# Decode attention with a gated feed-forward: tile slots numbered by the program, w_down in one load, sixteen single-partition loads on GpSimd's queue

## The chip, the cores and the metric

One core of a Trainium2 chip runs the whole kernel. The metric is the device time of one execution in microseconds; the median of three runs is given, and beside it one execution that was taken with the hardware profiler.

## What is computed

One token attends over a cache of 65,536 keys and values in each of 32 heads, and a feed-forward of the same token is mixed in with a gate:

```
q = x @ wq                        # x: 1 x 512, wq: 512 x 4096, 32 heads of 128
p = softmax(q . k_cache / sqrt(128))     # k_cache: 32 x 65536 x 128, bf16
a = (p @ v_cache) @ wo            # wo: 4096 x 512
b = (silu(x @ w_gate) * (x @ w_up)) @ w_down    # 512 x 1792, 1792 x 512
g = sigmoid(sum(x * gate_w))
out = g * a + (1 - g) * b
```

The two caches are 1,073.7 MB of the 1,087.6 MB that the kernel reads from HBM.

## The kernel before, in words

**Tiles.** A head's keys are cut into G = 4 tiles of 128 x 128 positions, so there are N = 128 K tiles and as many V tiles, of 4 MiB each: 128 partitions with 32 KB each, contiguous in HBM. They live in the pool `ring` (L58), which has SLOTS = 5 buffers under one tag; `big` (L69) takes the next one. The same five slots first hold wq (L77), K0, K1, w_gate with w_up (L132) and w_down (L136), and at the end the second half of wo (`load_wo_end`, L157). The first half of wo comes in four groups of four heads from a pool of its own (`load_wo`, L164).

**Engines.** For a K tile, DVE multiplies it in place by the query, which is broadcast along the positions (L240), and halves the products three times by adding (L244) down to 16 columns; `scores` (L249) sums those on PE with 16 matmuls against an identity (L254). After a head's four tiles come the maximum (L266 to L275), the exponentials on ACT (L279) and their total (L288). `values` (L296) multiplies a V tile by the probabilities in 32 matmuls of 4 columns each (L302). `head_column` (L320) turns a head's result into a column, and `project` (L334) multiplies it by its 128 rows of wo into a_ps.

**Order.** It is written out by hand. `steps` (L344) pairs each K tile n with a V tile v: v starts four tiles behind n and from n = 40 on falls back to eight behind. In a step the program issues the load of K tile n and then that of V tile v, both on SP's queue, then DVE's products of K tile n, and on PE, in this order, the column of a finished head, `values` of v, the total, `scores` of n, and the projection of a finished head. An engine carries out its instructions in that order, and SP issues a load only when what it waits for has come: the slot's earlier users, and an earlier load that used the same one of eight DMA semaphores. A DMA's semaphore is raised by one by each of the DMA engines that carry it, sixteen for a whole tile. The last steps hold V tiles only; the last two V tiles and the second half of wo are loaded in pieces, so that PE can begin on the first.

**Feed-forward.** `feed_forward_in` (L169) is issued in step 1, `feed_forward_mid` (L189) in step 2 and `feed_forward_out` (L218) in step 3. w_down lies in 64 partitions with 28 KB each. It comes in eight loads of eight rows, every fourth one (`load_wd`, L142): two of them stand ahead of the load of K2 on SP's queue, six behind it. The hidden vector is brought into the same 64-partition form by two matmuls (L202) and a copy (L206), and b_ps takes 28 matmuls (L209).

Of the kernel before, what the change touches and what calls it, by code (L numbers as in the profile page):

```python
# [8 lines left out]
ACT = mybir.ActivationFunctionType  # L9
ALU = mybir.AluOpType  # L10
AXIS = mybir.AxisListType
P = 128
# [3 lines left out]
NB = 128  # L16
SLOTS = 5
# [8 lines left out]
def kernel(  # L26
# [14 lines left out]
    nc = tc.nc  # L41
    bf16 = mybir.dt.bfloat16
    f32 = mybir.dt.float32

    _, H, Sk, Dh = A_k_cache.shape
    D = A_x.shape[2]
    F = B_w_gate.shape[1]
    KT = D // P
    FT = F // P
    G = Sk // (NB * P)  # L50
    NBH = Sk // P
    N = H * G
# [2 lines left out]
    scale = float(Dh) ** -0.5  # L55

    consts = ctx.enter_context(tc.tile_pool(name="consts", bufs=1))
    ring = ctx.enter_context(tc.tile_pool(name="ring", bufs=SLOTS))  # L58
    small = ctx.enter_context(tc.tile_pool(name="small", bufs=2))
    ppool = ctx.enter_context(tc.tile_pool(name="ppool", bufs=3))  # L60
    wo_pool = ctx.enter_context(tc.tile_pool(name="wo_pool", bufs=2))
# [3 lines left out]
    psum_m = ctx.enter_context(tc.tile_pool(name="psum_m", bufs=2, space=bass.MemoryType.PSUM))  # L65

    ctx.enter_context(tc.manual_schedule())

    def big(name):  # L69
        return ring.tile([P, NB * Dh], bf16, name=name, tag="big")  # L70


    xT = consts.tile([P, KT], bf16, name="xT")
    gwT = consts.tile([P, KT], bf16, name="gwT")
    with nc.allow_non_contiguous_dma(reason="small"):
        nc.scalar.dma_start(out=xT, in_=A_x[0, 0, :].rearrange("(p t) -> p t", t=KT))
    wq_t = big("wq_t")  # L77
    wq_sb = wq_t[:, : KT * H * Dh].rearrange("p (t f) -> p t f", t=KT)
    nc.sync.dma_start(out=wq_sb, in_=A_wq.rearrange("(p t) f -> p t f", t=KT))

    ident_f = consts.tile([P, P], f32, name="ident_f")
    make_identity(nc, ident_f[:])
    ident_b = consts.tile([P, P], bf16, name="ident_b")
# [15 lines left out]

    K_tiles, V_tiles, S_tiles, P_tiles, O_tiles = {}, {}, {}, {}, {}  # L100

    def load(dst, cache, n, name, cuts=(0, NB)):
        h, g = divmod(n, G)
        t = big(name)
        view = t.rearrange("p (j d) -> p j d", d=Dh)
        src = cache[0, h, g * NB * P : (g + 1) * NB * P, :].rearrange("(p j) d -> p j d", j=NB)
        for a, b in zip(cuts[:-1], cuts[1:]):
            nc.sync.dma_start(out=view[:, a:b, :], in_=src[:, a:b, :])
        dst[n] = view

    load(K_tiles, A_k_cache, 0, "K_t", (0, NB // 2, NB))
    load(K_tiles, A_k_cache, 1, "K_t")

    def queries(g):
        qg_ps = psum_m.tile([P, QG * Dh], f32, name="qg_ps", tag="misc")
# [13 lines left out]
        queries(g)  # L129


    gu_t = big("gu_t")  # L132
    wgu_sb = gu_t[:, : 2 * KT * F].rearrange("p (w t f) -> p w t f", w=2, t=KT)
    nc.sync.dma_start(out=wgu_sb[:, 0], in_=B_w_gate.rearrange("(p t) f -> p t f", t=KT))
    nc.sync.dma_start(out=wgu_sb[:, 1], in_=B_w_up.rearrange("(p t) f -> p t f", t=KT))
    wd_t = big("wd_t")  # L136
    HP = P // 2
    GT = F // HP
    wd_sb = wd_t[:HP, : GT * D].rearrange("p (t n) -> p t n", t=GT)
    wd_rows = B_w_down.rearrange("(p t) n -> p t n", t=GT)  # L140

    def load_wd(*which):  # L142
        for i in which:
            lo = (0, 1, 2, 3, 32, 33, 34, 35)[i]
            part = slice(lo, lo + 29, 4)
            nc.sync.dma_start(out=wd_sb[part], in_=wd_rows[part])

    with nc.allow_non_contiguous_dma(reason="small"):
        nc.sync.dma_start(out=gwT, in_=gate_w.rearrange("(p t) -> p t", t=KT))
    load_wd(0, 1)  # L150
    WG = 4
    wo_tiles = {}

    WH = H // 2
    wo_end = []

    def load_wo_end(cuts):  # L157
        t = big("wo_t")[:, : (H - WH) * D].rearrange("p (h n) -> p h n", n=D)
        rows = A_wo[WH * P :, :].rearrange("(h p) n -> p h n", p=P)
        for a, b in zip(cuts[:-1], cuts[1:]):  # L160
            nc.sync.dma_start(out=t[:, a:b, :], in_=rows[:, a:b, :])
        wo_end.append(t)

    def load_wo(g):  # L164
        wo_tiles[g] = wo_pool.tile([P, WG, D], bf16, name="wo_sb")
        rows = A_wo[g * WG * P : (g + 1) * WG * P, :]
        nc.sync.dma_start(out=wo_tiles[g], in_=rows.rearrange("(h p) n -> p h n", p=P))

    def feed_forward_in():  # L169

# [18 lines left out]
    def feed_forward_mid(gu_sb, eg):  # L189
        nc.vector.tensor_scalar_add(eg, eg, 1.0)  # L190
        nc.vector.reciprocal(eg, eg)
        hprod = consts.tile([P, FT], f32, name="hprod")
        nc.vector.tensor_tensor(out=hprod, in0=gu_sb[:, :FT], in1=eg, op=ALU.mult)
        hT = consts.tile([P, FT], bf16, name="hT")
        nc.vector.tensor_tensor(out=hT, in0=hprod, in1=gu_sb[:, FT:], op=ALU.mult)
        xg = consts.tile([P, KT], f32, name="xg")
        nc.vector.tensor_tensor(out=xg, in0=xT, in1=gwT, op=ALU.mult)
        xs = consts.tile([P, 1], f32, name="xs")
        nc.vector.tensor_reduce(out=xs, in_=xg, axis=AXIS.X, op=ALU.add)
        h_ps = psum_m.tile([HP, GT], f32, name="h_ps", tag="misc")  # L200
        for r in range(2):
            nc.tensor.matmul(  # L202
                h_ps[:, r * FT : (r + 1) * FT], lhsT=ident_b[:, r::2], rhs=hT, start=True, stop=True
            )
        h2 = consts.tile([HP, GT], bf16, name="h2")
        nc.scalar.activation(out=h2, in_=h_ps, func=ACT.Copy)  # L206
        b_ps = psum_m.tile([1, D], f32, name="b_ps", tag="misc")
        for t in range(GT):
            nc.tensor.matmul(  # L209
                b_ps, lhsT=h2[:, t : t + 1], rhs=wd_sb[:, t, :], start=(t == 0), stop=(t == GT - 1)  # L210
            )
        g_ps = psum_m.tile([P, 1], f32, name="g_ps", tag="misc")
        nc.tensor.matmul(g_ps, lhsT=ones_f, rhs=xs, start=True, stop=True)
        eg2 = consts.tile([P, 1], f32, name="eg2")
        nc.scalar.activation(out=eg2, in_=g_ps, func=ACT.Exp, scale=-1.0)
        return b_ps, eg2
# [13 lines left out]
    def products(n, a=0, b=NB):  # L230

        h = n // G
        K = K_tiles[n][:, a:b, :]
        qb = q_bc[:, h * Dh : (h + 1) * Dh]
        q_rep = bass.AP(
            tensor=qb.tensor,
            offset=qb.offset,
            ap=[list(qb.ap[0]), [0, b - a], [1, Dh]],
        )
        yield nc.vector.tensor_tensor(out=K, in0=K, in1=q_rep, op=ALU.mult)  # L240
        half = Dh
        while half > WIDTH:
            half //= 2
            yield nc.vector.tensor_tensor(  # L244
                out=K[:, :, 0:half], in0=K[:, :, 0:half], in1=K[:, :, half : 2 * half],
                op=ALU.add,
            )
# [97 lines left out]
    v = 0  # L345
# [8 lines left out]
    ff = done = tot_ps = None  # L354
    for n, v in steps:
        if n is not None and n > 1:
            load(K_tiles, A_k_cache, n, "K_t")
        if n == 2:
            load_wd(2, 3, 4, 5, 6, 7)
        if n == 3:  # L360
            load_wo(0)
        if v is not None:
            if v % (WG * G) == 2 * G and v // (WG * G) + 1 < WH // WG:
                load_wo(v // (WG * G) + 1)
            load(V_tiles, A_v_cache, v, "V_t", (0, NB) if v < N - 2 else (0, 64, NB) if v < N - 1 else (0, 32, 64, 96, 112, NB))
            if v == N - 1:
                load_wo_end((0, 4, 8, 12, 14, 16))
        if n == 2:
            ff = feed_forward_mid(*ff)
        halves = (0, NB // 2)  # L370
        vector = iter(()) if n is None else products(n)
        if n == 0:
            vector = (i for a in halves for i in products(n, a, a + NB // 2))
        top_of = None
        if n is None:
            top_of = H - 1 if S_tiles else None
        elif n % G == 0 and n > 0:
            top_of = n // G - 1
            vector = (i for a in halves for i in products(n, a, a + NB // 2))
        if top_of is not None:  # L380
            next(vector, None)
            mT_ps = row_max(top_of)
            next(vector, None)
            exponentials(top_of, mT_ps)
        for _ in vector:
            pass
        if n == 1:
            ff = feed_forward_in()
        if n == 3:
            feed_forward_out(*ff)  # L390
        if tot_ps is not None:
            weight(*tot_ps)
            tot_ps = None
        if done is not None:
            head_column(done, head_copy(done))
        if v is not None:
            values(v)
        if top_of is not None:
            tot_ps = top_of, total(top_of)
        if n is not None:  # L400
            scores(n)
        if done is not None and done < WH:
            project(done)
        done = v // G if v is not None and v % G == G - 1 else None
# [40 lines left out]
```

## Time and profile before

| what | us |
|---|---|
| median of three runs | 2533.54 (2533.16 to 2534.53) |
| the profiled execution's own time | 2534.51 |
| its span, first to last instruction | 2532.6 |
| DVE busy | 2175.5 |
| PE busy, matmuls | 1742.4 |
| ACT busy | 75.9 |
| GpSimd busy | 0.7 |

The page gives the busy time of each engine, the queues of the DMA engines with the share of the sixteen engines' time that their packets took, and the chain of work that ended last. q1 is the queue that SP issues to, q10 that of ACT, and q8 carries the instructions that the engines' sequencers fetch. GpSimd issues no DMA in this kernel. The page's mean rate is 430 GB/s. A table by stage gives the same for stretches of the span, and a timeline the instructions in order of time. In these a line such as `SPq L108` is the issue of a load by SP, not its transfer.

### The profile page before, as it was taken

To read this page: it belongs to the slowest core of one execution; us is meant where nothing else is said; L and a number is where in the kernel's file an instruction comes from. 1 tells how busy PE (TensorE), PEld (TensorE's weight loads), DVE (VectorE), ACT (ScalarE), POOL (GpSimd) and SP (SyncE) were. 2 spreads that over 40 slices of the span, in tenths; PEclk is the share of its full clock that TensorE was granted. 3 is DMA by queue.
4 is the path that set the end of the run, shared out by engine and by line. 5 is a ranking of instruction groups with operands and counts; after the bars stand their busy time and mean duration, and the time that the engine had idled before them with its cause. 6 is when DMAs were issued, how large, how long until landed. Compare 5 with 4: busy or idle time off the path is not lost.

```text
span 2532.6 us, 15260 instructions
## 1 busy us (share of the span) xinstructions
PE 1742.4 (69%) x6738; PEld 712.1 (28%) x6738; DVE 2175.5 (86%) x784; ACT 75.9 (3%) x207; POOL 0.7 (0%) x6
## 2 busy tenths in 40 slices
PE   4677666776677666676776677667666776677679
PEld 2222222222222222222222223222222232222223
DVE  7998888888888999998888888888888888888860
ACT  1000000000000000000000000000000000000000
POOL 0000000000000000000000000000000000000000
PEclk7677777777777676677777777777777777777779
DMA  9999999999999999999999999999999999999998
GB/s 415 433 433 430 433 433 433 432 430 435 432 432 434 431 433 432 432 433 433 432 434 433 432 434 433 432 432 434 432 431 434 433 430 434 434 431 433 434 432 339
DMA packets 42884, 1088.63 MB, mean 430 GB/s; under 512 B 4737, under 2 KB 8834, under 8 KB 9090
## 3 DMA queue, kind: packets, MB, share of 16 engines
q1 hardware_dynamic: 42674, 1087.66, 99.7%
q8 instruction: 53, 0.87, 0.1%
q14 instruction: 13, 0.11, 0.0%
q10 hardware_dynamic: 144, 0.00, 0.0%
HBM read 1087.64 MB, written 0.00 MB: 429 GB/s over the span
## 4 chain that ended last, share of the span: by engine, by line
DMA 68%; PE 22%; DVE 10%; issue 1%; ACT 0%; DVEq 0%; SPq 0%
DMA V_t<-in_A_v_cache_dram 61%; PE O_ps L302 20%; DMA K_t<-in_A_k_cache_dram 5%; DVE K_t L240 5%; DVE K_t L244 5%; PE S_ps L254 1%; DMA wo_t<-in_A_wo_dram 1%; DMA wq_t<-in_A_wq_dram 0%; PE qg_ps L117 0%; DVE m L266 0%; PE oh_ps L323 0%; PE a_ps L335 0%; PE a_ps L227 0%; ACT P_sb L279 0%; DVE top L275 0%
## 5 line engine op out<-in xcount | busy, mean ns | idle before, releaser
L302 PE MATMUL O_ps<-V_t,P_sb 128*4 128x512 bf16 x4096 | 1157.3, 453 | 496.8 <-DMA V_t<-in_A_v_cache_dram 494.3
L240 DVE TENSOR_TENSOR K_t<-K_t,q_bc 128x16384 bf16<-128x16384 bf16 (+1 forms) x160 | 1117.2, 6983 | 254.4 <-DMA K_t<-in_A_k_cache_dram 232.9
L244 DVE TENSOR_TENSOR K_t<-K_t 128x4096 bf16<-128x4096 bf16 (+3 forms) x480 | 1030.9, 2148 | 14.3
L302 PEld LDWEIGHTS <-P_sb 128*4 128x4 bf16 x4096 | 393.9, 97 | 1241.0 <-issue 897.5
L254 PE MATMUL S_ps<-K_t,ident_b 128*128 128x128 bf16 x2048 | 466.0, 394 | 107.0 <-DVE K_t L244 106.9
L254 PEld LDWEIGHTS <-ident_b 128*128 128x128 bf16 x2048 | 227.6, 115 | 330.0 <-issue 140.2
L323 PE MATMUL oh_ps<-ident_f,O_sb 4*128 4x1 f32 x256 | 57.9, 343 | 74.1 <-ACT O_sb L315 74.1
L323 PEld LDWEIGHTS oh_ps<-ident_f,O_sb 4*128 4x128 f32 x256 | 55.2, 314 | 83.7 <-ACT O_sb L315 78.9
L270 PE MATMUL mT_ps<-diag,ones_f 128*128 128x128 f32 x64 | 23.6, 468 | 79.8 <-ACT diag L268 79.8
L268 ACT ACTIVATE diag<-ident_f,m 128x128 f32<-128x128 f32 x32 | 12.8, 401 | 2099.3 <-DVE m L266 2099.3
L317 DVE COPY O_sb<-O_ps 4x256 f32<-4x256 f32 x1 | 0.4, 414 | 52.1 <-ACT O_sb L315 52.1
L270 PEld LDWEIGHTS mT_ps<-diag,ones_f 128*128 128x128 f32 x64 | 14.7, 285 | 95.6 <-ACT diag L268 95.6
L266 DVE TENSOR_REDUCE m<-S_ps 128x1 f32<-128x512 f32 x32 | 21.9, 683 | 7.4 <-PE S_ps L254 7.4
L315 ACT ACTIVATE O_sb<-O_ps 4x512 f32<-4x512 f32 (+1 forms) x32 | 18.1, 566 | 131.0 <-PE O_ps L302 131.0
L279 ACT ACTIVATE P_sb<-S_ps,bias 128x512 bf16<-128x512 f32 x32 | 22.0, 687 | 1.0
L117 PE MATMUL qg_ps<-wq_t,X_bc 128*128 128x512 bf16 x32 | 8.6, 436 | 13.2 <-DMA wq_t<-in_A_wq_dram 13.2
L293 DVE RECIPROCAL recip<-tot_ps 128x1 f32<-128x1 f32 x32 | 5.1, 160 | 12.2 <-PE tot_ps L288 12.2
L209 PE MATMUL b_ps<-wd_t,h 64*1 64x512 bf16 x28 | 12.1, 629 | 4.3 <-DMA K_t<-in_A_k_cache_dram 4.3
L288 PEld LDWEIGHTS tot_ps<-rowsum,ones_f 128*128 128x128 f32 x64 | 9.5, 188 | 14.0 <-issue 14.0
L288 PE MATMUL tot_ps<-rowsum,ones_f 128*128 128x1 f32 x64 | 12.2, 260 | 0.0
L330 ACT ACTIVATE oT<-oh_ps,rg 128x1 bf16<-128x1 f32 x32 | 8.4, 263 | 76.6 <-PE oh_ps L323 76.6
L227 PE MATMUL a_ps<-b_sb,ones_f 1*1 1x512 f32 x2 | 1.9, 1032 | 12.1 <-ACT b_sb L226 12.1
(42 smaller groups left out, 73.8 us busy)
## 6 DMA issues: line engine op xcount, KB each, us to landing
K_t<-in_A_k_cache_dram SPq DMA_DIRECT2D x127, 4096.0 KB, 35.3
V_t<-in_A_v_cache_dram SPq DMA_DIRECT2D x126, 4096.0 KB, 29.1
wq_t<-in_A_wq_dram SPq DMA_DIRECT2D x1, 4096.0 KB
K_t<-in_A_k_cache_dram SPq DMA_DIRECT2D x2, 2048.0 KB, 16.8
V_t<-in_A_v_cache_dram SPq DMA_DIRECT2D x2, 2048.0 KB
V_t<-in_A_v_cache_dram SPq DMA_DIRECT2D x3, 1024.0 KB, 29.4
wo_sb<-in_A_wo_dram SPq DMA_DIRECT2D x4, 512.0 KB, 17.3
gu_t<-in_B_w_gate_dram SPq DMA_DIRECT2D x1, 1792.0 KB
```

Of the source, the lines that this page charges most:

```text
L209: nc.tensor.matmul(b_ps, lhsT=h2[:, t : t + 1], rhs=wd_sb[:, t, :], start=(t == 0), stop=(t == GT - 1))
L240: yield nc.vector.tensor_tensor(out=K, in0=K, in1=q_rep, op=ALU.mult)
L244: yield nc.vector.tensor_tensor(out=K[:, :, 0:half], in0=K[:, :, 0:half], in1=K[:, :, half : 2 * half], op=ALU.add,)
L254: nc.tensor.matmul(S_tiles[h][:, g * NB : (g + 1) * NB], lhsT=ident_b, rhs=K_tiles[n][:, :, c], start=(c == 0), stop=(c == WIDTH - 1),)
L266: nc.vector.tensor_reduce(out=m, in_=S_tiles[h], axis=AXIS.X, op=ALU.max)
L268: nc.scalar.activation(out=diag, in_=ident_f, func=ACT.Copy, scale=m)
L270: nc.tensor.matmul(mT_ps, lhsT=ones_f, rhs=diag, start=True, stop=True)
L279: nc.scalar.activation(out=P_tiles[h], in_=S_tiles[h], func=ACT.Exp, bias=bias, scale=scale, accum_out=rowsum[:, h : h + 1],)
L288: nc.tensor.matmul(tot_ps, lhsT=ones_f, rhs=rowsum[:, h : h + 1], start=True, stop=True)
L302: nc.tensor.matmul(O_tiles[h], lhsT=P_tiles[h][:, g * NB + j : g * NB + j + 4], rhs=V_tiles[n][:, j : j + 4, :], start=(g == 0 and j == 0) ...
L315: nc.scalar.activation(out=O_sb[:, :cut], in_=O_ps[:, :cut], func=ACT.Copy)
L323: nc.tensor.matmul(oh_ps, lhsT=O_sb[:, c * Dh : (c + 1) * Dh], rhs=ident_f[0:4, c : c + 1], start=(c == 0), stop=(c == 3),)
```

## The change

The pool `ring` goes. In its place stands one tile of 5 x 32 KB a partition, and `big` hands out its five parts in turn, in the order of the calls. Waits now follow from which part of the tile an instruction reads or writes. w_down takes 128 partitions with 14 KB each in one load, which is issued behind the load of K2; the reshaping of the hidden vector goes, and b_ps takes 14 matmuls. wo's first group is loaded in step 6 in place of step 3. Of its second group, partitions 0 to 15 come in sixteen loads of one partition each (4 rows of 1 KB) on GpSimd's queue, with nothing to wait for but, from the ninth on, the landing of the eighth before it; SP loads the other 112 partitions where it loaded all of them. xT is loaded on SP's queue behind wq, gwT on ACT's queue in xT's place. The third last V tile is loaded in two halves.

```diff
-    ring = ctx.enter_context(tc.tile_pool(name="ring", bufs=SLOTS))
...
-    def big(name):
-        return ring.tile([P, NB * Dh], bf16, name=name, tag="big")
+    UNIT = NB * Dh
+    ring = consts.tile([P, SLOTS * UNIT], bf16, name="ring")
+    taken = []
+
+    def big():
+        u = len(taken) % SLOTS
+        taken.append(u)
+        return ring[:, u * UNIT : (u + 1) * UNIT]
...
-        nc.scalar.dma_start(out=xT, in_=A_x[0, 0, :].rearrange("(p t) -> p t", t=KT))
-    wq_t = big("wq_t")
+        nc.scalar.dma_start(out=gwT, in_=gate_w.rearrange("(p t) -> p t", t=KT))
+    wq_t = big()
     wq_sb = wq_t[:, : KT * H * Dh].rearrange("p (t f) -> p t f", t=KT)
     nc.sync.dma_start(out=wq_sb, in_=A_wq.rearrange("(p t) f -> p t f", t=KT))
+    with nc.allow_non_contiguous_dma(reason="small"):
+        nc.sync.dma_start(out=xT, in_=A_x[0, 0, :].rearrange("(p t) -> p t", t=KT))
...
-    wd_t = big("wd_t")
-    HP = P // 2
-    GT = F // HP
-    wd_sb = wd_t[:HP, : GT * D].rearrange("p (t n) -> p t n", t=GT)
-    wd_rows = B_w_down.rearrange("(p t) n -> p t n", t=GT)
-
-    def load_wd(*which):
-        for i in which:
-            lo = (0, 1, 2, 3, 32, 33, 34, 35)[i]
-            part = slice(lo, lo + 29, 4)
-            nc.sync.dma_start(out=wd_sb[part], in_=wd_rows[part])
-
-    with nc.allow_non_contiguous_dma(reason="small"):
-        nc.sync.dma_start(out=gwT, in_=gate_w.rearrange("(p t) -> p t", t=KT))
-    load_wd(0, 1)
+    wd_t = big()
+    wd_sb = wd_t[:, : FT * D].rearrange("p (t n) -> p t n", t=FT)
...
-        nc.sync.dma_start(out=wo_tiles[g], in_=rows.rearrange("(h p) n -> p h n", p=P))
+        rows = rows.rearrange("(h p) n -> p h n", p=P)
+        lo = 16 if g == 1 else 0
+        for p in range(lo):
+            nc.gpsimd.dma_start(out=wo_tiles[g][p : p + 1], in_=rows[p : p + 1])
+        nc.sync.dma_start(out=wo_tiles[g][lo:], in_=rows[lo:])
...
-        h_ps = psum_m.tile([HP, GT], f32, name="h_ps", tag="misc")
-        for r in range(2):
+        b_ps = psum_m.tile([1, D], f32, name="b_ps", tag="misc")
+        for ft in range(FT):
             nc.tensor.matmul(
-                h_ps[:, r * FT : (r + 1) * FT], lhsT=ident_b[:, r::2], rhs=hT, start=True, stop=True
-            )
-        h2 = consts.tile([HP, GT], bf16, name="h2")
-        nc.scalar.activation(out=h2, in_=h_ps, func=ACT.Copy)
-        b_ps = psum_m.tile([1, D], f32, name="b_ps", tag="misc")
-        for t in range(GT):
-            nc.tensor.matmul(
-                b_ps, lhsT=h2[:, t : t + 1], rhs=wd_sb[:, t, :], start=(t == 0), stop=(t == GT - 1)
+                b_ps,
+                lhsT=hT[:, ft : ft + 1],
+                rhs=wd_sb[:, ft, :],
+                start=(ft == 0),
+                stop=(ft == FT - 1),
             )
...
         if n == 2:
-            load_wd(2, 3, 4, 5, 6, 7)
-        if n == 3:
+            nc.sync.dma_start(out=wd_sb, in_=B_w_down.rearrange("(p t) n -> p t n", t=FT))
+        if n == 6:
             load_wo(0)
...
-            load(V_tiles, A_v_cache, v, "V_t", (0, NB) if v < N - 2 else (0, 64, NB) if v < N - 1 else (0, 32, 64, 96, 112, NB))
+            load(V_tiles, A_v_cache, v, (0, NB) if v < N - 3 else (0, 64, NB) if v < N - 1 else (0, 32, 64, 96, 112, NB))
```

More of the change, by code (lines that the diff above doesn't have):

```diff
@@ L100, with load @@
     K_tiles, V_tiles, S_tiles, P_tiles, O_tiles = {}, {}, {}, {}, {}
-    def load(dst, cache, n, name, cuts=(0, NB)):
+    def load(dst, cache, n, cuts=(0, NB)):
         h, g = divmod(n, G)
-        t = big(name)
+        t = big()
         view = t.rearrange("p (j d) -> p j d", d=Dh)
@@ L109, in load @@
         dst[n] = view
-    load(K_tiles, A_k_cache, 0, "K_t", (0, NB // 2, NB))
-    load(K_tiles, A_k_cache, 1, "K_t")
+    load(K_tiles, A_k_cache, 0, (0, NB // 2, NB))
+    load(K_tiles, A_k_cache, 1)
     def queries(g):
@@ L129 @@
         queries(g)
-    gu_t = big("gu_t")
+    gu_t = big()
     wgu_sb = gu_t[:, : 2 * KT * F].rearrange("p (w t f) -> p w t f", w=2, t=KT)
@@ L157, in load_wo_end @@
     def load_wo_end(cuts):
-        t = big("wo_t")[:, : (H - WH) * D].rearrange("p (h n) -> p h n", n=D)
+        t = big()[:, : (H - WH) * D].rearrange("p (h n) -> p h n", n=D)
         rows = A_wo[WH * P :, :].rearrange("(h p) n -> p h n", p=P)
@@ L356 @@
         if n is not None and n > 1:
-            load(K_tiles, A_k_cache, n, "K_t")
+            load(K_tiles, A_k_cache, n)
         if n == 2:
-            load_wd(2, 3, 4, 5, 6, 7)
-        if n == 3:
+            nc.sync.dma_start(out=wd_sb, in_=B_w_down.rearrange("(p t) n -> p t n", t=FT))
+        if n == 6:
             load_wo(0)
```

## The prediction

> **What bounds the kernel now.** I read the page first: shares, queues, the chain that ended last.
>
> ```profile
> PE 1742.4 (69%) x6738; PEld 712.1 (28%) x6738; DVE 2175.5 (86%) x784; ACT 75.9 (3%) x207; POOL 0.7 (0%) x6
> ...
> q1 hardware_dynamic: 42674, 1087.66, 99.7%
> q8 instruction: 53, 0.87, 0.1%
> ...
> DMA 68%; PE 22%; DVE 10%; issue 1%; ACT 0%; DVEq 0%; SPq 0%
> ```
>
> SP's queue (q1) fills the sixteen DMA engines for 99.7% of the span: the kernel is bound by bytes. All bytes stay in the change, so only three things can move: how evenly they lie on the sixteen engines, whether the queue runs dry, and the tail. Next, the table by stage of the end (columns: stretch, length, busy time of PE, PEld, DVE, ACT and POOL, PE clock, DMA share, GB/s).
>
> ```profile
> 2490.00:2500.00 10.00, 9.32 (x48) 4.09 (x47) 0.00 (x0) 0.85 (x2) 0.00 (x0) 1.00 0.99 425
> 2500.00:2510.00 10.00, 8.38 (x40) 3.24 (x39) 0.00 (x0) 0.00 (x0) 0.00 (x0) 1.00 0.97 411
> 2510.00:2520.00 10.00, 10.00 (x48) 3.96 (x47) 0.00 (x0) 0.00 (x0) 0.00 (x0) 1.00 0.85 326
> 2520.00:2530.00 10.00, 9.70 (x48) 4.00 (x45) 0.63 (x2) 0.64 (x2) 0.00 (x0) 1.00 0.33 96
> ```
>
> The rate sinks to 326 and then 96 GB/s while loads are still open: some engines have finished, others not. Who they are shows in the times at which the sixteen engines add their one to a DMA's semaphore (us after the first of them; worked out of the trace, one semaphore, four DMAs):
>
> ```
> at   61.45: 0 0 .1 .1 .3 .3 .4 .4 | 8.3 8.4 8.4 8.5 8.5 8.7 8.7 9.8
> at 1663.20: 0 .7 5.4 5.4 5.5 5.8 7.0 7.2 | 8.1 8.2 8.5 8.6 9.9 12.4 14.1 15.2
> at 2499.64: 0 0 6.8 6.8 6.9 7.1 7.4 7.8 8.4 8.5 8.5 8.5 9.1 12.7 15.6 16.6
> at 2523.82: 0 0 .1 .1 .2 .2 .2 .2 .2 .2 .2 .3 .3 .7 3.5 4.6
> ```
>
> Up to 41 us all sixteen agree within 0.7 us. Then w_down comes, 64 packets of 28,672 bytes at 1.062 us, and eight engines take eight each: 8.50 us. That is the step of 8.3, and it never closes, as no engine ever idles. On top, the 53 instruction packets of q8 delay the engine that carries one by 1.2 to 1.4 us; followed from set to set they come round on the same eight engines, six of the early group and two of the late one. Those two have both burdens, end 15.6 and 16.6 behind, and every tile waits for them. The tail shows what that does:
>
> ```profile
> 2495.45 7.07 PE L302 MATMUL O_ps<-V_t,P_sb 128*4 128x512 bf16 x32
> 2504.14 20.88 PE L302 MATMUL O_ps<-V_t,P_sb 128*4 128x512 bf16 x96 [1.62 <-DMA V_t<-in_A_v_cache_dram]
> 2525.07 1.02 PE L335 MATMUL a_ps<-wo_t,oT 128*1 128x512 bf16 x4
> 2526.02 1.05 PE L323 MATMUL oh_ps<-ident_f,O_sb 4*128 4x1 f32 x8
> 2527.00 2.75 PE L335 MATMUL a_ps<-wo_t,oT 128*1 128x512 bf16 x12
> ```
>
> PE waits 1.62 us for tile V125 to land on the last engine, then works to 2529.75 without a hole. The slow engines' last wo piece lands at 2529.1: both paths end together, both hang on the slowest engine.
>
> **The change part by part.**
>
> w_down whole. The eight strided loads go; one load of 128 rows of 14,336 bytes comes, eight packets for each of sixteen engines. Packets of that size stand in the trace (w_gate, w_up): 0.535 us, so 4.28 us an engine. Late group: 4.28 - 8.50 = -4.22; early group +4.28. The slowest late engine goes from 16.6 to 12.4; the most delayed early ones from 8.5 to 12.8 (9.1 and 13.4 if that one is of this group). New worst 12.8: **-3.8 us** (bounds -3.2 and -4.2). Seven semaphore writes of 9 ns less on the late group: nothing. b_ps (L209: 28 matmuls, 12.10 us) becomes 14, about 6 us, and starts once w_down lands, near 55 instead of 60; h_ps and a copy go. That stage's PE work hides behind DVE's K products, which start as K2 lands: 53.2 instead of 54.0.
>
> The tail. Everything lands 3.8 us earlier, so V125 at 2500.3. Uncut, PE would follow at once and also end 3.8 earlier. Cut in two, V125's first half is there at 2495.5, and PE goes on from V124 without the 1.62 us hole; the wo pieces then bind, at 2525.3. Added gain 0 to 0.4; I take 0. The clock is granted in full in all four rows above, and DVE is as idle there as before.
>
> Slots by the program. By the built programs, a V load now takes the slot of an older K tile and waits for its scores (L254); before it took a V slot and waited for `values` (L302). A K load now follows the V load ahead of it at once. Each V load is thus issued later by the time from the end of `values` to the end of `scores`: 3.7 to 8 us in the rows I read. What covers this is the queue: a K load lands 35.3 us after its issue (median), 19.4 of them being itself and the V load ahead of it, so some 16 us of transfers are open when the V load is issued. Cost 0. The thin place is the first one:
>
> ```profile
> 107.05 0.33 SPq L108 DMA_DIRECT2D V_t<-in_A_v_cache_dram  x1
> ...
> 111.39 0.33 SPq L108 DMA_DIRECT2D K_t<-in_A_k_cache_dram  x1
> ```
>
> V2, issued at 107.05, will wait for what releases the row at 111.39, near 110.5 with the 0.8 gained. By the order of the queue (45.25 MiB up to K6, then wo's first group, which now stands there) the engines run dry at 114.3 at the earliest; a first packet comes 1.2 us after its issue (wq: 0.74 to 1.95). Margin 2.6 us, cost 0. If `values` ran wholly at the half clock seen up to 101.7, 32 x 0.43 = 13.8 us instead of 8.75, it would be 2.5 us of stall: I keep +2.5 for the range.
>
> xT behind wq. It lands at about 13.4 instead of 8.39, X_bc takes 0.63, so the query matmuls start near 14.1 instead of 13.23; K2's load, queued on SP behind their wait, goes out near 22.7 instead of 21.86. Its cover is gate and up, in transfer until 41.1. gwT on ACT's queue is first read at 53. Cost 0. wo's first group moves past four loads and is read at 182: 0.
>
> Sixteen single partitions. SP's load of group 1 loses 4 of 32 packets of 1 KB an engine (46 ns each): -0.18 us. GpSimd's sixteen loads carry 64 such packets: spread, +0.18; nothing waits ahead of them and PE first reads the group at 495.4, far behind. The trace has no load on this queue. Low end: 46 ns a packet. High end: what a foreign queue's packet costs here, the instruction packet's 1.4 us, all sixteen on the same four engines: 22.4 us there. I take 0, as the packets are 1 KB like wo's own.
>
> [...]
>
> Sum: the profiled execution took 2534.51 (span 2532.6 and 1.9 around it); minus 3.8 is 2530.7. It was 0.97 above the median of 2533.54, so **2529.7** in the terms of the runs.
>
> **Rivals.**
>
> *The gain is larger.* If the instruction packets fell on all sixteen engines (3.3 each, 4.6 us) instead of eight (7 each, 9.3 us), the worst engine gains 4.6 more: 2525.1. For it: another program with another queue in use. Against: the same engines all through this trace.
>
> *The gain is given back.* The thin place at 110 stalls, or tiles wait elsewhere for scores, on all engines at once: 2532 to 2533.5. Against: 16 us of cover later on.
>
> *It does not even the engines out.* If w_down's 128 rows, or the 112 of wo, lay on fewer engines than I count, the worst stays: 2533.5. Against: every 128-row load here adds its sixteen ones.
>
> *Slower.* The sixteen singles, in the first tens of us, pile up on four engines at up to 1.4 us a packet. Such an engine, if it carries no instruction packets, has 12.8 - 2.7 = 10 us of slack after the change, so this costs from 0.63 us a packet on, and passes the bound for slower from 1.2; at 1.4 it is 2529.7 + 12.4 = 2542.1. Against: 1 KB each.
>
> **How the numbers follow.** About 0.2% (5.1 us) is what a measurement of this kernel can tell from no change, so 2528.5 and 2538.6 are the bounds. My forecast: 0.55, own range 2528.0 to 2531.2, of it 0.07 beyond the bound. Larger gain 0.18, of it 0.17 faster. Given back 0.14 and not evened out 0.05: same. Slower 0.08. Faster 0.24, same 0.68, slower 0.08. The range goes from the larger gain's 2525 to 2534.5; the slower case is left out.
>
> **What would show it.** Right: the sixteen increments stay within 0.7 us after w_down and end some 9 to 10 apart instead of 16.6; eight engines, not two, come last; PE has no hole ahead of V125; the tail's rate falls later and more steeply. Wrong: a dip of the DMA share near 112 us (slots); GpSimd's packets far over 46 ns or on few engines (singles); instruction packets on other engines; a last stage in which PE, not wo, ends last.

## The result, and the profile after

The changed kernel took **2543.29 us** in the median of five runs (2542.90 to 2543.94); the kernel before took 2534.53 beside it (2533.16 to 2536.08). The ratio is 1.0036, with a 95% interval of 1.0024 to 1.0047. The change made the kernel 8.8 us slower, where 3.8 us less had been forecast. The profiled execution took 2543.74, its span 2541.9.

From the page of the kernel after: busy times, the queues and the shares of the chain that ended last.

```profile
PE 1732.1 (68%) x6722; PEld 708.6 (28%) x6722; DVE 2175.4 (86%) x784; ACT 75.7 (3%) x206; POOL 9.1 (0%) x22
...
q1 hardware_dynamic: 42770, 1087.59, 99.8%
q8 instruction: 52, 0.85, 0.1%
q0 software_dynamic: 512, 0.07, 0.0%
...
DMA 58%; PE 27%; DVE 14%; issue 1%; ACT 0%; SPq 0%; DVEq 0%
```

SP's queue fills the DMA engines as before, 99.8%, and no engine of the core has become busier but GpSimd, by 8.4 us, with its queue q0. So the queue did not run dry. Where the time went shows in the middle of the span, in the table by stage (stretch, length, busy time of PE, PEld, DVE, ACT and POOL, PE clock, DMA share, GB/s), first of the kernel before, then of the kernel after:

```profile
1200.00:1600.00 400.00, 281.00 (x1061) 113.11 (x1061) 348.24 (x124) 10.58 (x30) 0.00 (x0) 0.75 1.00 433
```

```profile
1200.00:1600.00 400.00, 275.12 (x1035) 110.50 (x1035) 349.48 (x123) 10.58 (x30) 0.00 (x0) 0.75 1.00 431
```

The DMA share is 1.00 in both, but 433 GB/s have become 431. A queue that is never dry and moves less has longer packets. The trace has each of them. The two columns are the mean time of a packet, and the time from the start of one packet to the start of the next on the same engine, 300 to 2400 us into the span. The trace does not name a packet's engine; a packet was taken to follow the one that ends as it starts. Packets that an instruction packet held up are left out; with them the second column is 1210.4 and 1214.5:

```
              32 KB packet   start to start
before        1213.0 ns      1209.4 ns
after         1216.9 ns      1213.4 ns
```

In the kernel before, 32,361 of the 32,512 packets of 32 KB take exactly 1213 ns. In the kernel after nearly all take 1213 to 1228. 4.0 ns on eight packets an engine for each 4 MiB, over 1037.2 MiB, are 8.3 us: two thirds of the 12.6 us between the forecast change, -3.8, and the measured one, +8.8.

The end of the kernel after, by stage and as a timeline of PE (start, length, engine, line, operation, count, idle time ahead and what ended it):

```profile
2510.00:2520.00 10.00, 10.00 (x48) 3.98 (x47) 0.00 (x0) 0.00 (x0) 0.00 (x0) 1.00 1.00 418
2520.00:2530.00 10.00, 9.11 (x43) 3.49 (x42) 0.00 (x0) 0.00 (x0) 0.00 (x0) 1.00 0.79 316
2530.00:2540.00 10.00, 8.50 (x41) 3.48 (x39) 1.09 (x2) 0.64 (x2) 0.00 (x0) 1.00 0.52 184
```

```profile
2504.82 17.43 PE L298 MATMUL O_ps<-ring,P_sb 128*4 128x512 bf16 x80
2523.14 7.07 PE L298 MATMUL O_ps<-ring,P_sb 128*4 128x512 bf16 x32 [0.89 <-DMA ring<-in_A_v_cache_dram]
2530.50 3.61 PE L298 MATMUL O_ps<-ring,P_sb 128*4 128x512 bf16 x16 [0.29 <-DMA ring<-in_A_v_cache_dram]
2534.42 1.02 PE L331 MATMUL a_ps<-ring,oT 128*1 128x512 bf16 x4 [0.31 <-DMA ring<-in_A_wo_dram]
...
2536.35 2.75 PE L331 MATMUL a_ps<-ring,oT 128*1 128x512 bf16 x12
```

Counted from the end of the span, the rate now falls later and more steeply, as forecast, and PE runs through V125: the row at 2504.82 is V124, V125 and the first half of V126. The increments of one DMA at 2506.30 end 11.9 us apart where they ended 16.6 apart, and nine engines are late, not two. The evener ends that were to make the gain are there; something else took the gain and 8.8 us more.

### The profile page after: what moved, and what is told of

It reads as the page before. It is cut to its first block, busy times and chain, and to the rows that moved or that the text cites. A ratio compares the mean times of both kernels' runs of the same rounds, so it can differ in the third digit from the quotient of the medians.

```text
span 2541.9 us, 15156 instructions
## 1 busy us (share of the span) xinstructions
PE 1732.1 (68%) x6722; PEld 708.6 (28%) x6722; DVE 2175.4 (86%) x784; ACT 75.7 (3%) x206; POOL 9.1 (0%) x22
## 3 DMA queue, kind: packets, MB, share of 16 engines
q1 hardware_dynamic: 42770, 1087.59, 99.8%
## 4 chain that ended last, share of the span: by engine, by line
DMA 58%; PE 27%; DVE 14%; issue 1%; ACT 0%; SPq 0%; DVEq 0%
DMA ring<-in_A_v_cache_dram 53%; PE O_ps L298 19%; PE S_ps L250 8%; DVE ring L236 7%; DVE ring L240 6%; DMA ring<-in_A_k_cache_dram 5%; DMA ring<-in_A_wo_dram 1%; DVE m L262 0%; PE oh_ps L319 0%; PE a_ps L331 0%; PE a_ps L223 0%; ACT P_sb L275 0%; DVE top L271 0%; SPq L115 0%; ACT O_sb L311 0%
## 5 line engine op out<-in xcount | busy, mean ns | idle before, releaser
L298 PE MATMUL O_ps<-ring,P_sb 128*4 128x512 bf16 x4096 | 1155.1, 452 | 515.1 <-DMA ring<-in_A_v_cache_dram 512.9
L236 DVE TENSOR_TENSOR ring<-ring,q_bc 128x16384 bf16<-128x16384 bf16 (+1 forms) x160 | 1117.3, 6983 | 257.0 <-DMA ring<-in_A_k_cache_dram 257.0
L240 DVE TENSOR_TENSOR ring<-ring 128x4096 bf16<-128x4096 bf16 (+3 forms) x480 | 1031.0, 2148 | 14.3
L250 PE MATMUL S_ps<-ring,ident_b 128*128 128x128 bf16 x2048 | 465.7, 394 | 112.4 <-DVE ring L240 112.4
L124 PE MATMUL qg_ps<-ring,X_bc 128*128 128x512 bf16 x32 | 9.1, 455 | 15.0 <-DVE X_bc L98 15.0
```

The costliest lines, as they stand in the source:

```text
L124: nc.tensor.matmul(qg_ps, lhsT=X_bc[:, t, :], rhs=wq_sb[:, t, g * QG * Dh : (g + 1) * QG * Dh], start=(t == 0), stop=(t == KT - 1),)
L240: yield nc.vector.tensor_tensor(out=K[:, :, 0:half], in0=K[:, :, 0:half], in1=K[:, :, half : 2 * half], op=ALU.add,)
L250: nc.tensor.matmul(S_tiles[h][:, g * NB : (g + 1) * NB], lhsT=ident_b, rhs=K_tiles[n][:, :, c], start=(c == 0), stop=(c == WIDTH - 1),)
L298: nc.tensor.matmul(O_tiles[h], lhsT=P_tiles[h][:, g * NB + j : g * NB + j + 4], rhs=V_tiles[n][:, j : j + 4, :], start=(g == 0 and j == 0) ...
```

## The experiments

**The theories.** A: the slots' place in a partition. The change was to number five slots by hand; it also moved them. By the addresses in the two built programs, the pool's slots began at byte 30976 of a partition, 121 times 256; the five are 32,768 bytes apart, so each of them began on a multiple of 256. The one tile `ring` begins at byte 16512, which is 128 past a multiple of 256. B: GpSimd's queue q0, used by its sixteen loads, slows the DMA engines for good. C: DMA engines that run closer in step get in one another's way. A kernel that differs from the kernel after by 128 unused bytes tells A from both, and so does the kernel before with those bytes.

**Ring on a multiple of 256.**

```diff
+    pad = consts.tile([P, 64], bf16, name="pad")
+    nc.vector.memset(pad, 0.0)
     UNIT = NB * Dh
     ring = consts.tile([P, SLOTS * UNIT], bf16, name="ring")
```

> The kernel after, with one unused 128-byte tile ahead of the ring, so that the ring's start moves from byte 16512 of a partition (128 past a multiple of 256) to 16640 (a multiple of 256). Nothing else changes. Theory A (the place of the tiles in a partition makes each 32 KB packet 4 to 5 ns longer, 255 tiles x 8 packets): packets back at 1213 ns, a tile's period back at 9.68 us, about 8 us gone, so 2535 us or up to 2 less. Theory B (GpSimd's single loads and their queue slow the engines for good): packets stay at 1213 to 1227 ns, mean 1218, time stays at 2543. Theory C (engines that run closer in step get in one another's way): as B, 2543.

Measured: 2533.59 us (before 2534.52 beside it). The ratio to before, 1.0010 (0.9992 to 1.0027), is widened by two of its eleven runs, at 2548.65 and 2555.26; the other nine lie between 2532.96 and 2533.73. The same row of the table by stage of this kernel:

```profile
1200.00:1600.00 400.00, 279.37 (x1062) 112.85 (x1062) 348.21 (x124) 10.57 (x30) 0.00 (x0) 0.76 1.00 433
```

433 GB/s again, and packets of 1213.0 ns. 128 bytes that nobody reads give back 9.7 us. The unused tile moves every tile behind it too, but the packets that get shorter are those of the ring. B and C fall as causes of the long packets: GpSimd's loads and the narrow spread are both still there.

**The kernel before, its slots moved off.** The same tile of 128 bytes, ahead of xT; the slots begin at 31104.

> The kernel before, with the same unused 128-byte tile ahead of its slots, so that they start 128 bytes past a multiple of 256 instead of on one. Theory A: packets of 1213 to 1227 ns, a tile every 9.71 us, about 8 us slower, 2542. Theories B and C: nothing of the change is in this kernel, so 2534.5 as the kernel before, and packets of 1213 ns.

Measured: 2544.65 us (2543.36 to 2544.78), ratio 1.0039 (1.0025 to 1.0052), 10.1 us more than before. Its row:

```profile
1200.00:1600.00 400.00, 273.94 (x1033) 110.27 (x1033) 349.53 (x122) 10.58 (x30) 0.00 (x0) 0.75 1.00 431
```

Nothing of the change is in this kernel but the place of its slots, and it has the loss: packets of 1216.9 ns, 431 GB/s. A is shown from both sides. Its price was put at 8 from packet times, and 4.0 ns from start to start give 8.3; measured are 9.7 and 10.1. Part of the rest is on the engines that come last. With the ring off the multiple an instruction packet takes 1073 ns in the median, with it on the multiple 934, and near 2500 us the last increment comes 11.9 us after the first instead of 10.8 (the kernel after against the one with the ring moved). For the kernel before, whose ends are not closer with the slots on the multiple (16.6 us against 15.8 off it), the other 1.8 us stay open.

**Without the sixteen single loads, ring where the change put it.**

```diff
-        lo = 16 if g == 1 else 0
-        for p in range(lo):
-            nc.gpsimd.dma_start(out=wo_tiles[g][p : p + 1], in_=rows[p : p + 1])
-        nc.sync.dma_start(out=wo_tiles[g][lo:], in_=rows[lo:])
+        nc.sync.dma_start(out=wo_tiles[g], in_=rows)
```

> The kernel after without the sixteen single loads: SyncE's queue loads all 128 partitions of wo's second group at once; the ring stays 128 bytes past a multiple of 256. Theory A: packets stay at a mean of 1218 ns; only what the singles cost in the first 25 us comes back, about 1.2 us, so 2542. Theory B: packets back at 1213 ns, 2530 to 2535. Theory C: packets stay long, 2542.

Measured: 2540.50 us (2540.38 to 2540.72), ratio 1.0025 (1.0015 to 1.0034). Packets stay long, so A again; but 2.8 us come back, not 1.2. The singles cost more than the 1.2 us expected of them.

**Both: ring on a multiple of 256, no single loads.**

> The kernel after with the ring on a multiple of 256 and without the sixteen single loads. Theory A: the packets of before and the narrower spread of the engines' ends together, so 2530, give or take 2: below the kernel before by what w_down as a whole was forecast to save (3.8), less what xT's place costs at the start. Theory B: 2530 to 2535 as well, told apart by e1 and e3. Theory C (the spread narrower, so packets longer): 2542.

Measured: 2530.71 us (2530.45 to 2530.88), ratio 0.9985 (0.9976 to 0.9993). This beats both kernels, the one before by 3.8 us. That is the gain that was forecast, with neither the singles nor the moved ring in it.

**Where the 2.8 us go.** The times at which the queue has delivered so many MiB, of the kernel with the ring moved (it has the singles) against the last one (it has not), averaged over 4 MiB around each point, stand 0.7 us apart at 8 MiB, 0.7 at 91, and 3.0 at 100 MiB and at 1000. So most is lost at one place, near 230 us, where SP loads wo's second group. Two rows of the kernel without singles, then of the one with them, both on 256:

```profile
226.00:230.00 4.00, 4.00 (x16) 1.44 (x15) 3.23 (x2) 0.00 (x0) 0.00 (x0) 0.79 0.95 403
230.00:234.00 4.00, 4.00 (x20) 1.74 (x18) 2.04 (x1) 0.00 (x0) 0.00 (x0) 1.00 1.15 470
```

```profile
226.00:230.00 4.00, 4.00 (x13) 1.32 (x12) 3.93 (x3) 0.00 (x0) 0.00 (x0) 0.64 0.97 414
230.00:234.00 4.00, 4.00 (x19) 1.60 (x18) 0.13 (x1) 0.00 (x0) 0.00 (x0) 1.00 0.99 228
```

228 GB/s in place of 470, at a share of about 1 in both: the engines are busy and move half. (Over so short a stretch, where a packet counts at its start, both figures are rough.) In the first, the load of 128 partitions, the 1 KB packets take 46 ns each; in the second, of 112, they take 82 in the median, and 32 KB packets beside them up to 2.3 us instead of 1.21. GpSimd's own 1 KB packets were over by 24 us. To take GpSimd out of it, the kernel without singles was given the same cut on SP's queue:

```diff
-        nc.sync.dma_start(out=wo_tiles[g], in_=rows)
+        lo = 16 if g == 1 else 0
+        if lo:
+            nc.sync.dma_start(out=wo_tiles[g][:lo], in_=rows[:lo])
+        nc.sync.dma_start(out=wo_tiles[g][lo:], in_=rows[lo:])
```

> The kernel with the ring on a multiple of 256 and no GpSimd loads (2530.71), wo's second group loaded by SyncE's queue in two loads, partitions 0 to 15 and 16 to 127. Theory D (the load of 112 partitions is what costs: in the kernel after and with the ring moved its 1 KB packets took 80 to 85 ns instead of 46 and the 32 KB packets beside them up to 2.3 us, and 2.5 us were lost between 228 and 240 us): the same dent there, 2533.2. Theory B2 (the loss there comes from GpSimd's queue in use): no dent, 2530.9.

Measured: 2532.98 us (2532.56 to 2533.54), ratio 0.9995 (0.9986 to 1.0004): 2.3 us more than with one load of 128, and the dent is there:

```profile
230.00:234.00 4.00, 4.00 (x20) 1.77 (x18) 0.00 (x0) 0.00 (x0) 0.00 (x0) 1.00 1.06 242
```

D holds: the cut into 16 and 112 costs 2.3 with no load on GpSimd's queue. The remaining 0.6 (2533.59 less 2532.98) fall to the sixteen single loads there; the runs of the two kernels overlap, but 0.7 is also what the singles had cost by 8 MiB. Is it the uneven seven partitions an engine? The same with `cut = 64`:

> The kernel with the ring on a multiple of 256 and no GpSimd loads (2530.71), wo's second group loaded by SyncE's queue in two loads of 64 partitions, 0 to 63 and 64 to 127, instead of one of 128. [...] Theory Q (only counts that do not divide evenly, seven partitions an engine, are slow): packets of 46 ns, 2530.7. [...]

Measured: 2533.63 us (2532.65 to 2534.19), ratio 0.9996 (0.9987 to 1.0005), so 2.9 more than one load of 128; 1 KB packets of 81 ns in the median, and the dent is the same:

```profile
230.00:234.00 4.00, 4.00 (x20) 1.86 (x18) 0.60 (x1) 0.00 (x0) 0.00 (x0) 1.00 1.12 251
```

Q falls: 64 partitions divide evenly and are as slow. That there are two loads instead of one is not it either: in a run below nearly all tiles come in two loads of 128 partitions, at 0.04 us a tile. Why the cut loads are slow is not shown: the trace names neither the engine nor the partition of a packet. What is shown is that one load of 128 has 1 KB packets of 46 ns, that 16 and 112 cost 2.3 us more (82 ns for the 112 in the kernel with the ring moved), and 64 and 64 2.9 (81 ns).

**What the place costs: by distance or once?** In the kernel without singles the pad was cut to 64 bytes (ring 192 past a multiple of 256) and raised to 192 (ring 64 past).

> The kernel with the ring on a multiple of 256 and without single loads (2530.71), its ring moved to start 192 bytes past a multiple of 256. At 128 past, the same kernel took 2540.50, 9.8 us more. Theory A1 (a packet pays for the bytes from the boundary below up to its start): cost in proportion to the offset, 9.8 x 192/128 = 14.7 us, 2545.4, packets of 1213 + 7 ns. Theory A2 (a packet pays once for not starting on the boundary, whatever the distance): 2540.5, packets as at 128. Theory A3 (what matters is the distance to the nearest boundary, or a multiple of 64 is enough): 2535.6, or 2530.7. [...]

Measured: 2540.03 us (2539.82 to 2540.19), ratio 1.0022 (1.0013 to 1.0031); packets of 1216.6 ns.

> The same kernel with the ring 64 bytes past a multiple of 256. Theory A1: 9.8 x 64/128 = 4.9 us, 2535.6, packets of 1213 + 2.5 ns. Theory A2: 2540.5. Theory A3: 2535.6 by the nearest boundary (told apart from A1 by 192), 2530.7 if a multiple of 64 is enough.

Measured: 2540.92 us (2540.73 to 2541.08), ratio 1.0027 (1.0016 to 1.0037); packets of 1216.8 ns.

So at 64, 128 and 192 past, the kernel takes 2540.92, 2540.50 and 2540.03, and on the multiple 2530.71. A2: the price does not grow with the distance, and a multiple of 64 is not enough. A1 would have made 192 three times as dear as 64, 14.7 us against 4.9; measured are 9.3 and 10.2.

Once for each packet, or a share of the bytes? In the kernel after, packets of 32, 16, 8 and 4 KB take 3.9, 2.5, 4.0 and 1.7 ns more on average, which speaks for the packet but not cleanly. So nearly all tiles were loaded in two halves, first on a multiple of 256:

```diff
-    def load(dst, cache, n, cuts=(0, NB)):
+    def load(dst, cache, n, cuts=(0, NB // 2, NB)):
...
-            load(V_tiles, A_v_cache, v, (0, NB) if v < N - 3 else (0, 64, NB) if v < N - 1 else (0, 32, 64, 96, 112, NB))
+            load(V_tiles, A_v_cache, v, (0, 64, NB) if v < N - 1 else (0, 32, 64, 96, 112, NB))
```

> The kernel with the ring on a multiple of 256 and no GpSimd loads (2530.71), every K and V tile but the last V tile loaded in two halves, so that nearly all packets are of 16 KB. It is the control for the next one. A 16 KB packet takes 611 ns here, two of them 1222 instead of 1213: 9 ns x 8 x 256 tiles, 18 us more, 2549; theories A2 and A4 say the same of it.

Measured: 2541.75 us (2541.70 to 2541.93), ratio 1.0029 (1.0018 to 1.0041): 11.0 us more than whole tiles, not 18. The packet's duration was the wrong row. From start to start two halves take 2 x 607.1 = 1214.1 ns against 1209.4; 4.7 ns x 8 x 256 tiles are 9.6 us, and one more semaphore packet for each load and engine, 5.9 ns from start to start, makes 1.5: 11.1.

> As the control (halves), but with the ring 192 bytes past a multiple of 256. Theory A2 (a packet pays once for starting off the boundary, 4 to 5 ns whatever its size): twice the packets, so about 19 us over the control. Theory A4 (the cost is a share of the bytes, 0.4 per cent): 9.5 us over the control, as with whole tiles.

Measured: 2559.34 us (2559.18 to 2559.75), ratio 1.0099 (1.0085 to 1.0113): 17.6 us over the control. With whole tiles the same offset cost 9.3 (2540.03 less 2530.71). Twice the packets, 1.9 times the price, and again 4.0 ns more a packet from start to start (611.1 against 607.1): A2. A4 falls.

**w_down alone.** In the kernel before, only w_down comes in one load (14 matmuls, no reshaping), with 64 unused bytes for those that the removed tile had taken, so that the slots stay at 30976.

> The kernel before with w_down whole as its only change: one load of 128 partitions behind the load of K2, 14 matmuls, no reshaping; 64 unused bytes keep the slots on a multiple of 256. Theory S (the 3.8 us between the kernel before and the kernel with the ring on 256 and without singles are the evener load of the sixteen engines): 2530.7, spread of the last increments about 10 us instead of 16.6. Rival (they come from the slots' order, xT's place or V125 in halves): 2534.5.

Measured: 2530.51 us (2530.36 to 2530.64), ratio 0.9985 (0.9976 to 0.9994), 4.0 us less than before. Its increments end 10.1 us apart. Theory S holds, and no other part of the change shows a gain. Its tail on PE:

```profile
2500.38 20.88 PE L287 MATMUL O_ps<-V_t,P_sb 128*4 128x512 bf16 x96 [1.36 <-DMA V_t<-in_A_v_cache_dram]
2521.09 1.03 PE L320 MATMUL a_ps<-wo_t,oT 128*1 128x512 bf16 x4
...
2523.03 2.75 PE L320 MATMUL a_ps<-wo_t,oT 128*1 128x512 bf16 x12
```

The hole ahead of V125 is still there, and the whole tail has moved 3.8 to 4.0 us forward.

**The account**, from medians, each step a pair of kernels that differ by it. (The kernel before, run beside them each time, took 2534.5 to 2534.6, so kernels of different rounds can be set side by side.)

| step | us | from |
|---|---|---|
| w_down whole | -4.0 | before to w_down alone |
| slots' order, xT behind wq, V125 in halves, wo's first group later | +0.2 | w_down alone to ring on 256 without singles |
| wo's second group as 16 and 112 partitions | +2.3 | to the cut on SP's queue |
| the 16 singly, on GpSimd's queue | +0.6 | to ring on 256 with singles |
| ring at byte 16512 instead of 16640 | +9.7 | to the kernel after |
| sum | +8.8 | measured: +8.8 |

The steps of 0.2 and 0.6 are smaller than the spread of the runs on either side of them.

## Why the prediction was wrong, step by step

**w_down whole** was right. Forecast -3.8 with bounds of -3.2 and -4.2, measured -4.0 where it is the only change. There the spread of the ends came out at 10.1 where 9 to 10 had been named (11.9 in the kernel after), and from set to set the late engines fall back in steps of some 1.3 us (in the kernel after mostly 1.3 to 1.8, about every 48 us), as by the instruction packets, which come as often there (43 from 300 to 2400 us). The rival of a larger gain, these packets on all sixteen engines, did not come.

**The tail** was right: V125 in halves adds nothing that shows (it is part of the +0.2). PE has no hole ahead of V125, as forecast; it has 0.89 us ahead of the second half of V126 instead. PE then waits 0.31 us for wo's first piece and goes on without a hole, so the wo pieces bind, as forecast.

**Slots by the program** is the step that failed: "Cost 0". As to the waits, it was right. V2's load had been expected near 110.5. It goes out at 112.40 (at 110.46 with the ring on the multiple and without singles), and a K load 0.4 behind it. From the kernel after, the two loads and the table by stage at this thin place:

```profile
112.40 0.33 SPq L115 DMA_DIRECT2D ring<-in_A_v_cache_dram  x1
112.83 0.38 SPq L115 DMA_DIRECT2D ring<-in_A_k_cache_dram  x1
```

```profile
108.00:112.00 4.00, 4.00 (x21) 2.03 (x19) 4.00 (x2) 0.00 (x0) 0.00 (x0) 0.91 0.95 410
112.00:116.00 4.00, 4.00 (x14) 1.23 (x13) 4.00 (x1) 0.00 (x0) 0.00 (x0) 0.67 1.04 404
```

The DMA share stays near 1, and from 95 to 130 us sixteen packets are in transfer at every moment: the queue did not run dry, and the rival in which the gain is given back did not come. But the step counted only who waits for whom. Behind it stands the sentence near the start of the prediction, that all bytes stay, so "only three things can move": evenness, a dry queue and the tail. The time of a packet was a fourth, and it was put at nothing without a reason. The step did not ask where the five parts of the new tile lie. The two built programs gave the addresses; the trace of the kernel before has nearly all its 32 KB packets at one duration, with all slots on a multiple of 256, so it had no row for another place, and the range needed a bound for one. The missing term is 4.0 ns x 8 x 259, 8.3 us by that working and 9.7 as measured.

**xT behind wq** was right as to cost. It landed later than worked out, at about 14.6 instead of 13.4, and K2's load went out at 24.10 (23.56 without the singles) instead of 22.7; gate and up covered that.

**Sixteen single partitions** failed as well, at the half that looked harmless. GpSimd's 1 KB packets took 48.0 ns on average, as wo's own 46 had suggested, they were over by 24 us, and the sixteen loads cost 0.6 us. The remainder on SP's queue was put at -0.18 us, four packets fewer at 46 ns each. Its packets took 82 to 86 ns in the median, and the tiles' packets beside them were longer too: +2.3 us for the cut. No row of the kernel before shows a load of 112, so the -0.18 was the author's estimate; the prediction priced that load only for lying on fewer engines than sixteen, and its semaphore takes sixteen ones in the kernel after (234.1 to 237.9 us). A price for "another shape of load on the same engines" was the place for a bound.

**The slower rival** named 2542.1, close to what came, but by luck. Its mechanism did not occur: the longest 1 KB packet of the singles took 88 ns, not 1.4 us, and behind them, at 37 us, the sixteen increments lie within 1.3 us, where 22 had been added up for four engines. The range ended at 2534.5 because the step with most of the loss had been taken as a matter of waits alone, and the other had no bound.

## What to carry to other kernels

In a kernel that is bound by its DMA queue, as this one is, an edit that moves a tile in SBUF can be an edit of the transfer time, here by 9.7 us: read the start of each large tile from the built program, before and after, and keep it on a multiple of 256 bytes, which is worth 0.4% of the time here. A small tile declared ahead of a large one was enough to lose it (10.1 us in the kernel before), and 128 unused bytes were enough to mend it (9.7 us). If the DMA share stays at 1.00 and GB/s falls, as here from 433 to 431, look at the packets, not at the waits; and take their price from start to start (two halves 4.7 ns more than a whole tile's packet), not from their duration (9), and over a long stretch: in 40 us, some 530 packets, one that is held up by 490 ns, the mean in the kernel before, moves the mean by 0.9 ns. Do not cut a load by partitions to shift a few bytes: the rest of the load may cost more than the piece, here 2.3 us against 0.6.

## What the runs showed of the hardware that was not expected

In these kernels a 32 KB packet into SBUF took 1209.4 ns from start to start when its destination began on a multiple of 256 bytes, and 1213.4 to 1213.5 when it began 64, 128 or 192 past one; the time lost with the ring 64, 128 or 192 past is nearly the same, 9.3 to 10.2 us of 2530.7. It was paid for each packet: 17.6 us with halves, 9.3 with whole tiles. The instruction packets, too, took longer with the ring off the multiple, 1073 ns in the median in place of 934.

A load of wo's group (512 KB, 1 KB pieces) in the stream of tiles left no dent as one load of 128 partitions (403 and 470 GB/s in the two rows from 226 to 234 us); as 16 and 112 it cost 2.3 us more, and as 64 and 64 2.9. The tiles' packets beside the cut loads were slow as well, up to 2.3 us beside the 112, and 2.6 beside the two loads of 64, in place of 1.21.
